# An opening stage written out in source order, with the weights loaded and converted earlier

## The chip, the cores and the metric

The kernel runs on one core of a Trainium2 chip. The metric is the time of one execution on the device, in microseconds (us). The core has five engines with a queue of instructions each: PE (the matrix engine), DVE (the vector engine), ACT (the scalar engine), POOL (the general engine) and SP, which here issues most of the DMA transfers. The engines run side by side and wait for one another by semaphores.

## The reference, cut to what matters

There are four batches of 12480 tokens of width 128. In each, 49 agent vectors attend to the keys and collect the values, and then each query attends to the 49 agents. The result, 49920 rows of 128, goes through a gated feed-forward layer of 2048 units.

```python
a2k = softmax(scale * agents @ k.T)        # 49 x 12480, per batch
agent_v = a2k @ v                          # 49 x 128
q2a = softmax(scale * q @ agents.T)        # 12480 x 49
x = (q2a @ agent_v).reshape(49920, 128)
h = x @ w_in                               # 128 -> 2048, weights in 64-bit floats
g = h * (1.0 / (1.0 + np.exp(-1.702 * h)))
out = (g @ w_out).astype(np.float32)       # 2048 -> 128
```

The weights come as 64-bit floats. [...]

## The kernel before, in words

**The main loop.** The tokens are taken 1000 at a time, in 50 groups; a group has 16 steps, one for each 128 units of the feed-forward layer. `two_steps(t)` does steps t and t+1: `up` (L437, L440) multiplies the softmax of the queries with a product of agent values and `w_in`, ACT applies the activation (L450), `high` rounds the result (a DMA cast issued by POOL, L456, or ACT or DVE), `low` takes the rest on DVE (L465), and `down` (L475), four steps later, multiplies both with `w_out`. Beside this, a table `at` holds jobs with the step at which each is due: for the next batches the loads, splits and scores of the keys and values, and for the next groups those of the queries. In the main loop PE, ACT, DVE and POOL carry out their work in the order of the source; only the SP queue is ordered by a planner, which takes, in the order of the source, what it holds to be ready.

**The opening.** Before the loop, the first batch has to be worked through, since the loop needs its agent values. Its order on all engines is the planner's. The keys come in 13 blocks of 960 tokens (L578) and get scored (`first_key_scores`, L236), ACT copies the scores out (L245), DVE keeps a running maximum (L252). `do_query_split` makes three 16-bit parts of the first 1000 queries on DVE (L183, L185). Then the maximum over all keys is taken (L259 to L276, with two transposes on PE), and it is subtracted from the scores block by block (`key_shift`, L291: the first on DVE, the twelve others on POOL), ACT takes the exponent (L295), and PE sums up the values (L616). The 13 blocks of values go into buffers that later hold weights; there is room for eight blocks, and each two more wait until the sums have read the buffer they go into. Scores, softmax and transposes of the first queries are `do_query_scores`, `do_query_shift`, `do_query_exp`, `do_query_sums`, `do_query_softmax`, `do_query_pairs` (L380 to L427).

**The weights.** `load_words` brings a block of 512 columns in 64-bit form, 512 KB, into one of three buffers that keys and values use later (tag `kv`); four blocks of `w_in` and four of `w_out` are needed. `to_float32` makes floats of a block by eight operations on DVE (L133 to L145). For `w_out`, ACT then makes a rounded copy (L154) and DVE the rest (L155). The buffer is free for the next block once the sixth operation has read it. `weights_part` (L350) multiplies the agent values with a block of `w_in`; ACT copies the product (L357), DVE takes the rest (L359), and six small DMA transfers (`move`, L366) put the rest where `up` wants it.

**What is in which order before.** SP issues the 13 key blocks, the first queries, two value blocks, the first `w_in` block, the eleven other value blocks, and then the other weights. The block of `w_in` that came in first is converted while POOL shifts the scores; the other seven are converted after the value sums and among the first steps of the main loop.

Of the kernel before, what the change touches and what calls it, by code (L numbers as in the profile page):

```python
# [35 lines left out]
V_AT = (6, 10, 14)  # L36
V_SLOTS = (3, 2, 2, 2, 2, 2)
R = 30
FIRST_WORDS = 1
FIRST_UP = 2  # L40
BOTH = (0,)
ON_DVE = (2,)
EPS = 1e-09
# [3 lines left out]
def kernel(  # L47
# [77 lines left out]
    def to_float32(w, out=None):  # L125
        lo = w[:, :, 0]
        hi = w[:, :, 1]
        ts = nc.vector.tensor_scalar
        stt = nc.vector.scalar_tensor_tensor

        tmp = work.tile([P, 2, 512], U32, name="tmp", tag="rest")
        ex = tmp[:, 0].bitcast(I32)
        ts(out=ex.bitcast(U32), in0=hi, scalar1=20, scalar2=0x7FF, op0=ALU.logical_shift_right, op1=ALU.bitwise_and)  # L133
        ts(out=ex, in0=ex, scalar1=1023 - 127, scalar2=1023 + 128, op0=ALU.max, op1=ALU.min)
        ts(out=ex, in0=ex, scalar1=float(127 - 1023), scalar2=float(1 << 23), op0=ALU.add, op1=ALU.mult)
        stt(out=ex.bitcast(U32), in0=hi, scalar=0x80000000, in1=ex.bitcast(U32), op0=ALU.bitwise_and, op1=ALU.bitwise_or)

        m = work.tile([P, 512], U32, name="m21", tag="o")
        r = tmp[:, 1]
        ts(out=m, in0=hi, scalar1=0xFFFFF, scalar2=0x100000, op0=ALU.bitwise_and, op1=ALU.bitwise_or)  # L140
        ts(out=r, in0=lo, scalar1=8, scalar2=None, op0=ALU.logical_shift_right)
        stt(out=m.bitcast(F32), in0=m, scalar=float(1 << 24), in1=r, op0=ALU.mult, op1=ALU.add)
        if out is None:
            out = m.bitcast(F32)
        stt(out=out, in0=m.bitcast(F32), scalar=2.0**-44, in1=ex.bitcast(F32), op0=ALU.mult, op1=ALU.mult)  # L145
        return out

    def up_weights(i, w):
        to_float32(w, w_in_sb[:, i * 512 : (i + 1) * 512])

    def down_weights(i, w):
        s = slice(i * 4, (i + 1) * 4)
        wo = to_float32(w).rearrange("p (f c) -> p f c", c=C)
        nc.scalar.copy(out=wo_h[:, s, :], in_=wo)  # L154
        nc.vector.tensor_sub(out=wo_l[:, s, :], in0=wo, in1=wo_h[:, s, :].bitcast(F32))  # L155

# [74 lines left out]
    def first_key_scores(g, kt):  # L231

        for c in range(2):
            ps = ps_m.tile([P, 512], F32, name="ps_m")
# [11 lines left out]
        running_max(g, score[:TB, g * KB : (g + 1) * KB, :])  # L246

    def running_max(g, s):
        if g == 0:
# [12 lines left out]
    def key_max_1(d):  # L262
        mx = d["mx"]
        ps = ps_m.tile([P, 512], F32, name="ps_m")
# [7 lines left out]
    def key_max_2(d):  # L272
        mrow = d["mrow"]
        ps = ps_m.tile([P, 512], F32, name="ps_m")
# [3 lines left out]
    def key_max():  # L278
        d = {}
        key_max_0(d)  # L280
        key_max_1(d)
        key_max_2(d)

    def value_load(b, g):
        t = loads.tile([P, KB, C], F32, name="vt", tag="kv")
# [64 lines left out]
    def weights_part(b, w, c):  # L350
        if c == 0:
            wts[b] = wpool.tile([P, F], F32R, name="wh"), wpool.tile([P, F], F32R, name="wq")
        wh, wq = wts[b]
        s = slice(c * 512, (c + 1) * 512)
        pw = ps_m.tile([P, 512], F32, name="ps_m")
        nc.tensor.matmul(out=pw, lhsT=w["avT"], rhs=w_in_sb[:, s], start=True, stop=True)  # L356
        nc.scalar.copy(out=wh[:, s], in_=pw)  # L357
        wl = work.tile([P, 512], F32R, name="wl")
        nc.vector.tensor_sub(out=wl[:A], in0=pw[:A], in1=wh[:A, s].bitcast(F32))  # L359
        move(wh[A:H, s], wl[0 : R // 2])  # L360
        move(wh[H + A : P, s], wl[R // 2 : R])
# [190 lines left out]
    def do_query_exp(n):  # L552
        if n < NG:
            query_exp(scored[n])
# [22 lines left out]
    for g, t in enumerate(first_keys()):  # L577
        nc.sync.dma_start(out=t, in_=kT[0, :, g * KB : (g + 1) * KB, :])  # L578
        kts[0, g] = t
    do_query_load(0)  # L580
    words_in = []
    for g in range(NKG):
        if g % 2 == 0:
            vt0 = wpool.tile([P, 2, KB, C + 1], F32, name="vt0", tag=("wh", "wq")[g // 2 % 2])
            nc.gpsimd.memset(vt0[:, :, :, C :], 1.0)
        vts[0, g] = vt0[:, g % 2]
        nc.sync.dma_start(out=vt0[:TB, g % 2, :, 0:C], in_=v[0, :, g * KB : (g + 1) * KB, :])
        if g == FIRST_WORDS:
            words_in.append(load_words(w_in, 0))
    words = []  # L590
    for i in range(NF // 4):
        if i:
            words_in.append(load_words(w_in, i))
        words.append(load_words(w_out, i))
    for g in range(NKG):
        first_key_scores(g, kts.pop((0, g)))
    for i in range(4):
        do_query_split(0, i)
    key_max()
    def ahead(n):  # L600
        for c in range(2):
            do_query_scores(n, c)
        do_query_load(n + 1)
        do_query_shift(n)
        do_query_exp(n)
        do_query_sums(n)

    ahead(0)
    do_query_softmax(0)
    acc_ps = ps_o.tile([P, 512], F32, name="po0")  # L610
    for g in range(NKG):
        key_shift(g, nc.vector.tensor_tensor if g == 0 else nc.gpsimd.tensor_tensor)
        key_exp(g, 1)
# [9 lines left out]
        if g == FIRST_UP:  # L623
            up_weights(0, words_in[0])
        if g == 6:
            do_query_pairs(0)
    accs[0] = work.tile([P, 2 * C + 1], F32, name="acc", bufs=1)
    nc.gpsimd.memset(accs[0], 0.0)
    nc.vector.tensor_copy(out=accs[0][:A, 0:C], in_=acc_ps[:A, 0:C])
    nc.vector.tensor_copy(out=accs[0][:A, 2 * C :], in_=acc_ps[:A, C : C + 1])  # L630
    w0 = {}
    weights_0(accs.pop(0), w0)
    weights_1(w0)
    for c in range(2):
        if c:
            up_weights(c, words_in[c])
        weights_part(0, w0, c)
    for i in range(4):
        do_query_split(1, i)
    ahead(1)  # L640
    do_query_softmax(1)
    down_weights(0, words[0])


    steps = NG * NF
# [11 lines left out]
        pe_steps.add(t)  # L657
        return t

    for i in range(1, NF // 4):  # L660
        if i > 1:
            put(4 * i - 8, lambda i=i: up_weights(i, words_in[i]))
            put(pe_step(4 * i - 6), lambda i=i: weights_part(0, w0, i))
        put((1, 4, 6)[i - 1], lambda i=i: down_weights(i, words[i]))
    exps = {}
    for b in range(B - 1):
        s0 = due[b] - due[b] % (2 * NF) if b else 0
        done = s0
        for k in range(NKG):
            t = s0 + (K_AT if b else K_FIRST)[k]  # L670
            assert pe_step(t) == t
            put(t - 13 if b else max(t - 13, 0), lambda b=b, k=k: do_key_load(b + 1, k))
# [53 lines left out]
        put(s0 + Q_AT + 1, lambda n=n: do_query_shift(n + 2))  # L726


    E = mybir.EngineType
    g = {}  # L730
    gh = {}
    gl = {}
# [51 lines left out]
    def do_low(u):  # L784
        gl[u] = low(g.pop(u), gh[u])

    with tc.manual_schedule(engines={E.PE, E.Activation, E.DVE, E.Pool}):
        for t in range(0, steps + LAG, 2):
            two_steps(t)
    assert not at  # L790


# [36 lines left out]
```

## Time and profile before

| what | value |
|---|---|
| time, median of 3 runs | 2001.62 us (2001.57 to 2003.75) |
| the profiled execution's own time | 1999.4 us |
| its span in the profile | 1997.6 us |
| busy: PE, DVE, ACT, POOL | 1954.9 (98%), 1628.0 (81%), 1425.6 (71%), 270.0 (14%) us |
| chain of work that ended last, by engine | PE 90%, DVE 4%, issue 3%, DMA 2% |
| first `up` of the main loop begins | 76.17 us |

Times in the profile count from the start of the span. A busy PE is not a PE at its peak. The granted clock is given as a share of full speed: 1.00 is 2.4 GHz and 0.50 is 1.2 GHz. From about 122 us on PE is busy almost without a gap; what comes before is the opening and the first steps of the main loop.

### The profile page before, as it was taken

The numbers are of one execution on the slowest core, as the hardware profiler recorded it, in microseconds if no ns is written. First come the engines' busy times: TensorE is split into PE (matmuls) and PEld (weight loads), VectorE is DVE, ScalarE is ACT, GpSimd is POOL, SyncE is SP. The second block draws the span as 40 slices with busy tenths as digits, with TensorE's granted clock in tenths as the row PEclk, the third lists the DMA queues.
The fourth block names the chain that finished last, engine by engine and source line by source line (L and its number), as shares of the span: only waits on it lengthen the run. The fifth ranks groups of instructions, "written<-read, shape, count | busy, mean of one in ns | idle before, by whom it ended". The sixth has DMA issues, their size and how long they took to land.

```text
span 1997.6 us, 33834 instructions
## 1 busy us (share of the span) xinstructions
PE 1954.9 (98%) x12464; PEld 1472.8 (74%) x12464; DVE 1628.0 (81%) x2069; ACT 1425.6 (71%) x2364; POOL 270.0 (14%) x574
## 2 busy tenths in 40 slices
PE   8689999999999999999999999999999999999999
PEld 7467777777777777777777777777777777777776
DVE  5799989888788889888879888988877767777675
ACT  3267777777767776776777777677777787777875
POOL 3011111111111111111111111111111111111111
PEclk9799999999999999999999999999999999999999
DMA  9556666655556665665546566565445555554543
GB/s 264 179 166 186 191 188 191 173 182 190 168 181 193 182 182 178 201 179 175 180 161 198 184 200 183 173 194 177 151 160 171 163 174 162 166 168 162 181 145 134
DMA packets 132777, 356.26 MB, mean 178 GB/s; under 512 B 15984, under 2 KB 60992, under 8 KB 132612
## 3 DMA queue, kind: packets, MB, share of 16 engines
q0 software_dynamic: 64928, 230.58, 35.3%
q1 hardware_dynamic: 67684, 123.52, 22.5%
q8 instruction: 98, 1.61, 0.3%
q14 instruction: 67, 0.55, 0.1%
HBM read 81.01 MB, written 25.56 MB: 53 GB/s over the span
## 4 chain that ended last, share of the span: by engine, by line
PE 90%; DVE 4%; issue 3%; DMA 2%; ACT 0%; POOL 0%; SPq 0%; ACTq 0%; POOLq 0%; DVEq 0%
PE po L475 53%; PE ph L437 17%; PE ph L440 8%; PE ps_m L196 3%; PE ps_m L310 2%; PE ps_m L410 1%; PE ps_m L236 1%; PE ps_m L215 1%; DMA gh<-g 1%; DVE gl L465 1%; PE ps_m L217 1%; PE po L616 1%; PE ps_m L356 1%; PE ps_m L218 0%; PE ps_m L216 0%
## 5 line engine op out<-in xcount | busy, mean ns | idle before, releaser
L450 ACT ACTIVATE g<-ph 128x500 f32<-128x500 f32 x1600 | 811.1, 594 | 467.5 <-PE ph L440 463.1
L465 DVE TENSOR_TENSOR gl<-g,gh 128x1000 fp32r<-128x1000 f32 x800 | 939.9, 1195 | 124.9 <-DMA gh<-g 79.7
L475 PE MATMUL po<-gh,wo_h 128*128 128x500 f32 x1600 | 533.2, 414 | 1.4 <-DMA gh<-g 1.4
L475 PE MATMUL po<-gl,wo_h 128*128 128x500 f32 x1600 | 494.6, 390 | 2.9 <-DVE gl L465 2.8
L475 PE MATMUL po<-gh,wo_l 128*128 128x500 f32 x1600 | 492.6, 389 | 0.0
L456 POOL DMA_DIRECT2D gh<-g x450 | 241.0, 535 | 1657.3 <-ACT g L450 1108.9
L475 PEld LDWEIGHTS po<-gl,wo_h 128*128 128x128 f32 x1600 | 301.0, 189 | 68.7 <-DVE gl L465 7.2
L475 PEld LDWEIGHTS po<-gh,wo_l 128*128 128x128 f32 x1600 | 301.6, 188 | 62.0
L475 PEld LDWEIGHTS po<-gh,wo_h 128*128 128x128 f32 x1600 | 272.5, 189 | 87.8 <-issue 55.1
L437 PE MATMUL ph<-sa,wh 128*128 128x500 f32 x800 | 314.4, 393 | 5.2 <-ACT g L450 4.3
L460 ACT CAST gh<-g 128x1000 fp32r<-128x1000 f32 x300 | 309.5, 1032 | 8.9
L437 PE MATMUL ph<-sb,wh 128*128 128x500 f32 x800 | 314.2, 393 | 0.0
L440 PE MATMUL ph<-rq,wq 19*128 19x500 f32 x1600 | 201.1, 491 | 0.0
L437 PEld LDWEIGHTS ph<-sa,wh 128*128 128x128 f32 x800 | 150.7, 188 | 43.0 <-ACT g L450 12.4
L440 PEld LDWEIGHTS ph<-rq,wq 19*128 19x128 f32 x1600 | 76.6, 182 | 139.1 <-issue 139.1
L437 PEld LDWEIGHTS ph<-sb,wh 128*128 128x128 f32 x800 | 150.6, 188 | 37.8 <-ACT g L450 6.9
L185 DVE TENSOR_TENSOR rest<-rest 128x508 bf16<-128x508 f32 (+3 forms) x178 | 129.7, 737 | 0.9
L422 DVE TENSOR_TENSOR sa<-ps_m,sa 49x500 fp32r<-49x500 f32 x50 | 33.6, 672 | 54.4 <-ACT sb L420 54.3
L183 DVE TENSOR_TENSOR rest<-qt 128x508 f32<-128x508 f32 x100 | 67.5, 677 | 0.0
L218 PE MATMUL ps_m<-ag_part,rest 128*128 128x49 bf16 x400 | 59.9, 187 | 3.7 <-DVE rest L185 3.7
L450 ACT ACT_TABLE_LOAD x49 | 62.9, 1283 | 0.9
L486 ACT COPY o<-po 128x500 f32<-128x500 f32 x100 | 53.9, 608 | 13.3 <-PE po L475 12.8
(102 smaller groups left out, 1598.8 us busy)
## 6 DMA issues: line engine op xcount, KB each, us to landing
gh<-g POOLq DMA_DIRECT2D x450, 500.0 KB, 4.4
qt<-qT SPq DMA_DIRECT2D x100, 250.0 KB
kt<-kT SPq DMA_DIRECT2D x52, 480.0 KB
vt<-v SPq DMA_DIRECT2D x52, 480.0 KB
outT<-o SPq DMA_DIRECT2D x96, 250.0 KB
rq<-sa SPq DMA_DIRECT2D x100, 37.1 KB
rq<-sb SPq DMA_DIRECT2D x100, 37.1 KB
sa<-sa SPq DMA_DIRECT2D x100, 29.3 KB
```

The costliest lines, as they stand in the source:

```text
L183: nc.vector.tensor_sub(out=r[:, s], in0=t[:, s], in1=halves(t)[0][:, s])
L185: nc.vector.tensor_sub(out=halves(r)[1][:, s], in0=r[:, s], in1=halves(r)[0][:, s])
L196: nc.tensor.matmul(out=o, lhsT=x[:, t], rhs=ag_part[:, b, y, :], start=(i == 0), stop=(i == len(products) - 1),)
L218: mm(out=o[:, 0:A], lhsT=x2[:, t], rhs=a[:, 0:A], start=False, stop=True)
L437: nc.tensor.matmul(out=ph[k][:, :CH], lhsT=wts[c][0][:, cols[i]], rhs=pairs[c], start=True, stop=False)
L440: nc.tensor.matmul(out=ph[k][:, :CH], lhsT=wts[c][1][r, cols[i]], rhs=rq[r], start=False, stop=True, tile_position=(k * 32, 0),)
L450: nc.scalar.activation(out=gs[i][:, c, :], in_=ph[k][:, :CH], func=AF.Gelu_apprx_sigmoid)
L456: nc.gpsimd.dma_start(out=gh, in_=g)
L460: nc.scalar.copy(out=gh, in_=g)
L465: nc.vector.tensor_sub(out=gl, in0=g, in1=gh.bitcast(F32))
L475: nc.tensor.matmul(out=po[c][:, :CH], lhsT=lhsT[:, f, :], rhs=rhs[:, c, :], start=(begin and first), stop=(end and last),)
L486: nc.scalar.copy(out=o, in_=po[c][:, :CH])
```

## The change

- The opening is written out in source order for PE, ACT, DVE and POOL. SP's queue stays with the planner.
- Three weight blocks (`w_in` 0, `w_out` 0, `w_in` 1) are loaded among the first keys, the first queries after the sixth key block. Eight value blocks are asked for next. `w_out` 1, `w_in` 2 and `w_out` 2 follow where the source comes to them (in the key loop after block 6 and after block 10, and behind the key loop), the last two blocks after the first weight products.
- `to_float32` becomes a generator that stops after each operation; `convert(n)` does the next n of them. In the key loop two or three go ahead of each running maximum, in the value loop four after each of the last five blocks, and the rest at steps 0 to 2 of the main loop.
- The first queries are split after the last four key blocks. Their scores go ahead of the two transposes of the maximum on PE.
- All 13 shifts are on DVE, two blocks ahead of the sums. Split, scores and softmax of the second 1000 queries move into the value loop.
- The moves of the first two weight products are issued from ACT's queue; before, SP issued them, and POOL four of them.
- The third weight product is at step 0, ahead of the conversions of that step; the fourth stays at step 6. The first key loads of the next batch are due at step 4 at the earliest.

```diff
+WORDS_AT = (1, 4, 7)
+Q_FIRST = 5
+PART_AT = (0, 0, 0, 6)
+CONVERT_AT = (8, 8, 6, 6, 4, 4, 4, 4, 4, 4, 4)
...
+    def convert(ops):
+        while ops and converting:
+            if next(converting[0], 0) is None:
+                ops -= 1
+            else:
+                converting.pop(0)
...
+        queue = nc.scalar if b == 0 and c < 2 else None
+        move(wh[A:H, s], wl[0 : R // 2], queue)
+        move(wh[H + A : P, s], wl[R // 2 : R], queue)
         for i in range(4):
-            move(wq[i * 32 : i * 32 + A - R, s], wl[R:A], None if b or c else nc.gpsimd)
+            move(wq[i * 32 : i * 32 + A - R, s], wl[R:A], queue)
...
+    def load_next_words():
+        i, c = divmod(len(words), 2)
+        w = load_words((w_in, w_out)[c], i)
+        words.append(w)
+        converting.append((up_weights, down_weights)[c](i, w))
...
+    def shift(g):
+        key_shift(g, nc.vector.tensor_tensor)
+        key_exp(g, 1)
...
+    with tc.manual_schedule(engines=in_order):
...
+        for g, t in enumerate(first_keys()):
+            nc.sync.dma_start(out=t, in_=kT[0, :, g * KB : (g + 1) * KB, :])
+            kts[0, g] = t
+            if g in WORDS_AT:
+                load_next_words()
+            if g == Q_FIRST:
+                do_query_load(0)
+        values = first_values()
+        for g in range(KB):
+            next(values)
+        for g in range(NKG):
+            first_key_scores(g, kts.pop((0, g)))
+            convert(2 + g % 2)
+            running_max(g, score[:TB, g * KB : (g + 1) * KB, :])
+            if g == 6:
+                load_next_words()
+            if g == 10:
+                load_next_words()
+            if g >= NKG - 4:
+                do_query_split(0, g - NKG + 4)
+        do_query_load(1)
+        load_next_words()
+        d = {}
+        key_max_0(d)
+        for c in range(2):
+            do_query_scores(0, c)
+        key_max_1(d, ps_h.tile([P, 512], F32, name="ph"))
+        key_max_2(d, ps_h.tile([P, 512], F32, name="ph"))
+        shift(0)
+        shift(1)
+        do_query_shift(0)
+        do_query_exp(0)
+        acc_ps = ps_o.tile([P, 512], F32, name="po0")
+        for g in range(NKG):
+            if g + 2 < NKG:
+                shift(g + 2)
+            first_sums(g)
+            if g < 5 and g + KB < NKG:
+                next(values)
+            if g == 0:
+                do_query_sums(0)
+                do_query_softmax(0)
+            elif g < 5:
+                do_query_split(1, g - 1)
+                if g == 2:
+                    do_query_pairs(0)
+            elif g == 5:
+                for c in range(2):
+                    do_query_scores(1, c)
+                do_query_load(2)
+            elif g == 6:
+                do_query_shift(1)
+                do_query_exp(1)
+            elif g == 7:
+                do_query_sums(1)
+                do_query_softmax(1)
+            if g > 7:
+                convert(4)
+        nc.vector.tensor_copy(out=accs[0][:A, 0:C], in_=acc_ps[:A, 0:C])
...
+        for c in range(2):
+            weights_part(0, w0, c)
+        while len(words) < 8:
+            load_next_words()
...
+    for c in range(2, F // 512):
+        put(pe_step(PART_AT[c]), lambda c=c: weights_part(0, w0, c))
+    for t, ops in enumerate(CONVERT_AT):
+        put(t, lambda ops=ops: convert(ops))
```

## Rows read from the trace of the kernel before

**Rows 1.** Busy time of each engine in three stretches: the first keys, the values, and from there to the steady loop. Columns: stretch, its length, then for PE, PEld, DVE, ACT and POOL the busy us and the instructions, and at the end the granted clock, the DMA share and GB/s.

```profile
0.00:30.00 30.00, 24.35 (x208) 24.21 (x208) 10.22 (x22) 9.59 (x27) 3.49 (x17) 1.00 0.99 307
30.00:65.00 35.00, 26.91 (x246) 25.91 (x246) 23.78 (x39) 8.42 (x17) 14.21 (x16) 0.95 0.98 210
65.00:122.00 57.00, 39.47 (x195) 25.33 (x196) 49.93 (x89) 23.90 (x41) 6.30 (x14) 0.70 0.49 147
```

**Rows 2.** What SP issued in the opening, in order of time. Columns: start, us until the last of the group was issued, queue, line, operation, transfer, count.

```profile
1.18 9.17 SPq L578 DMA_DIRECT2D kt<-kT  x13
...
13.64 4.08 SPq L587 DMA_DIRECT2D vt<-v  x2
17.77 3.34 SPq L122 DMA_DIRECT2D words<-w_in  x1
21.15 26.97 SPq L587 DMA_DIRECT2D vt<-v  x11
48.16 2.47 SPq L122 DMA_DIRECT2D words<-w_out  x1
```

**Rows 3.** What the transfers moved in some stretches of the opening. Columns: stretch, its length, granted clock, DMA share (1 is all sixteen engines busy), GB/s.

```profile
10.00:18.00 8.00, 1.00 1.03 413
...
20.00:24.00 4.00, 1.00 1.17 211
...
28.00:50.00 22.00, 0.92 1.11 198
...
56.00:58.00 2.00, 1.00 0.98 383
```

**Rows 4.** Instructions of the opening in order of time. Columns: start, us, engine, line, operation, out<-in, shape, count, and in brackets how long the engine was idle before and what ended that.

```profile
0.74 0.39 SPq L85 DMA_DIRECT2D ag_sb<-agT  x1
...
2.75 0.93 DVE L162 CAST ag_part<-ag_sb 128x196 bf16<-128x196 f32 x1 [1.75 <-DMA ag_sb<-agT]
...
31.78 0.80 DVE L259 TENSOR_REDUCE mx<-run_max 120x49 f32<-120x392 f32 x1
...
33.87 0.22 PE L215 MATMUL ps_m<-ag_part,qt 128*128 128x98 bf16 x1
...
33.98 0.21 DVE L276 COPY max_b<-ps_m 120x49 f32<-120x49 f32 x1 [0.41 <-PE ps_m L275]
...
35.63 0.24 PE L218 MATMUL ps_m<-ag_part,rest 128*128 128x49 bf16 x1
36.36 13.13 PE L616 MATMUL po<-vt,score 120*49 120x129 f32 x112 [0.49 <-ACT score L295]
...
50.00 10.83 PE L616 MATMUL po<-vt,score 120*49 120x129 f32 x96
```

**Rows 5.** The chain that ended last, in order of time: one weight block of `w_out` from its first operation on DVE to the last, with the rest taken after ACT's copy. Columns: start, us, engine, tile, line.

```profile
93.45 0.35 DVE tmp L133
...
96.87 0.70 DVE m L145
97.60 0.63 ACT wo_h L154
98.25 0.69 DVE wo_l L155
```

**Rows 6.** The same chain: a running maximum, two pieces of a query split, and one of the operations on 125x392 of a query's softmax.

```profile
30.17 0.49 DVE run_max L252
30.66 1.23 DVE rest L185 x2
...
75.32 0.57 DVE e_sb L380
```

**Rows 7.** Instructions from the end of the value sums to the first activation, in order of time; columns as in rows 4.

```profile
64.95 0.28 DVE L629 COPY acc<-po 49x128 f32<-49x128 f32 x1
...
68.65 0.28 DVE L344 TENSOR_TENSOR avT<-ps_m,rz 128x128 f32<-128x128 f32 x1
...
71.82 0.68 DVE L359 TENSOR_TENSOR wl<-ps_m,wh 49x512 fp32r<-49x512 f32 x1 [0.96 <-ACT wh L357]
...
78.08 1.28 ACT L450 ACT_TABLE_LOAD   x1
...
79.37 2.02 ACT L450 ACTIVATE g<-ph 128x500 f32<-128x500 f32 x4
```

**Rows 8.** The line that issues the moves: what one issue takes on SP, ns min/median/max.

```profile
L366 SPq DMA_DIRECT2D wq<-wl x60: 564/572/865, 76.0 to 1496.6; - x60
L366 SPq DMA_DIRECT2D wh<-wl x32: 783/838/2061, 72.5 to 1490.1; - x32
```

**Rows 9.** PE in the main loop: the first matmul of `up` at steps 0, 6, 8, 12 and 22; columns as in rows 4.

```profile
76.17 0.47 PE L437 MATMUL ph<-sa,wh 128*128 128x500 f32 x1 [0.89 <-DMA wh<-wl]
...
94.09 0.39 PE L437 MATMUL ph<-sa,wh 128*128 128x500 f32 x1
...
109.62 0.39 PE L437 MATMUL ph<-sa,wh 128*128 128x500 f32 x1
...
121.93 0.39 PE L437 MATMUL ph<-sa,wh 128*128 128x500 f32 x1
...
145.89 0.38 PE L437 MATMUL ph<-sa,wh 128*128 128x500 f32 x1
```

**Rows 10.** DMA issues by line: the casts that POOL issues, count, KB each, median us from issue to landing.

```profile
gh<-g POOLq DMA_DIRECT2D x450, 500.0 KB, 4.4
```

More of the change, by code (lines that the diff above doesn't have):

```diff
@@ L145, in to_float32 @@
         stt(out=out, in0=m.bitcast(F32), scalar=2.0**-44, in1=ex.bitcast(F32), op0=ALU.mult, op1=ALU.mult)
+        yield
         return out
     def up_weights(i, w):
-        to_float32(w, w_in_sb[:, i * 512 : (i + 1) * 512])
+        yield from to_float32(w, w_in_sb[:, i * 512 : (i + 1) * 512])
     def down_weights(i, w):
         s = slice(i * 4, (i + 1) * 4)
-        wo = to_float32(w).rearrange("p (f c) -> p f c", c=C)
+        wo = yield from to_float32(w)
+        wo = wo.rearrange("p (f c) -> p f c", c=C)
         nc.scalar.copy(out=wo_h[:, s, :], in_=wo)
         nc.vector.tensor_sub(out=wo_l[:, s, :], in0=wo, in1=wo_h[:, s, :].bitcast(F32))
+        yield
+    words = []
+    converting = []
+    def convert(ops):
[4 more added lines that the diff above has]
+                converting.pop(0)
     ag_part = const.tile([P, B, 3, A], BF16, name="ag_part")
@@ L233, in first_key_scores @@
         for c in range(2):
-            ps = ps_m.tile([P, 512], F32, name="ps_m")
+            ps = ps_h.tile([P, 512], F32, name="ph")
             for j in range(KB // 2):
@@ L260, in key_max_0, with key_max_1 @@
         d["mx"] = mx
-    def key_max_1(d):
+    def key_max_1(d, ps=None):
         mx = d["mx"]
-        ps = ps_m.tile([P, 512], F32, name="ps_m")
+        if ps is None:
+            ps = ps_m.tile([P, 512], F32, name="ps_m")
         nc.tensor.transpose(out=ps[:A, :TB], in_=mx[:TB], identity=ident[:TB, :TB])
@@ L575, in first_keys, with first_values, first_sums @@
         return tiles[:NKG]
[L577 to L613, printed above, removed]
+    def first_values():
+        for g in range(NKG):
+            if g % 2 == 0:
+                vt0 = wpool.tile([P, 2, KB, C + 1], F32, name="vt0", tag=("wh", "wq")[g // 2 % 2])
+                nc.gpsimd.memset(vt0[:, :, :, C :], 1.0)
+            vts[0, g] = vt0[:, g % 2]
+            nc.sync.dma_start(out=vt0[:TB, g % 2, :, 0:C], in_=v[0, :, g * KB : (g + 1) * KB, :])
+            yield
+    def load_next_words():
[3 more added lines that the diff above has]
+        converting.append((up_weights, down_weights)[c](i, w))
+    def first_sums(g):
         vt = vts.pop((0, g))
@@ L622 @@
             )
[L623 to L630, printed above, removed]
-    w0 = {}
[L632 to L642, printed above, removed]
+    def shift(g):
+        key_shift(g, nc.vector.tensor_tensor)
+        key_exp(g, 1)
+    E = mybir.EngineType
+    in_order = {E.PE, E.Activation, E.DVE, E.Pool}
+    w0 = {}
+    with tc.manual_schedule(engines=in_order):
+        accs[0] = work.tile([P, 2 * C + 1], F32, name="acc", bufs=1)
+        nc.gpsimd.memset(accs[0], 0.0)
+        for g, t in enumerate(first_keys()):
[31 more added lines that the diff above has]
+        acc_ps = ps_o.tile([P, 512], F32, name="po0")
+        for g in range(NKG):
+            if g + 2 < NKG:
[23 more added lines that the diff above has]
+        nc.vector.tensor_copy(out=accs[0][:A, 0:C], in_=acc_ps[:A, 0:C])
+        nc.vector.tensor_copy(out=accs[0][:A, 2 * C :], in_=acc_ps[:A, C : C + 1])
+        weights_0(accs.pop(0), w0)
+        weights_1(w0)
+        for c in range(2):
+            weights_part(0, w0, c)
+        while len(words) < 8:
+            load_next_words()
@@ L658, in pe_step @@
         return t
[L660 to L664, printed above, removed]
+    for c in range(2, F // 512):
+        put(pe_step(PART_AT[c]), lambda c=c: weights_part(0, w0, c))
+    for t, ops in enumerate(CONVERT_AT):
+        put(t, lambda ops=ops: convert(ops))
     exps = {}
@@ L671 @@
             assert pe_step(t) == t
-            put(t - 13 if b else max(t - 13, 0), lambda b=b, k=k: do_key_load(b + 1, k))
+            put(t - 13 if b else max(t - 13, 4), lambda b=b, k=k: do_key_load(b + 1, k))
             begin = max(t - 4, done + 1)
@@ L785, in do_low @@
         gl[u] = low(g.pop(u), gh[u])
-    with tc.manual_schedule(engines={E.PE, E.Activation, E.DVE, E.Pool}):
+    with tc.manual_schedule(engines=in_order):
         for t in range(0, steps + LAG, 2):
             two_steps(t)
-    assert not at
+    assert not at and not converting
 _INS = ["qT", "kT", "v", "agT", "w_in", "w_out"]
```

23 lines of the change are left out of this document (10 added, 13 removed).

## The prediction

> **What bounds the kernel now.** I read first the share of the chain of waits and the granted clock along the span in the page, which say that from 122 us on PE is the limit; nothing of the change is there. Then the busy time by stretch [rows 1]. While the first keys are scored, PE is busy 24.4 of 30 us and DVE 10.2. From 65 to 122 us it is turned round: DVE is busy 49.9 of 57 us, PE 39.5 at a mean clock of 0.70. Two gaps of PE show the price: `up` of step 6 begins at 94.09 and that of step 8 at 109.62 us, where later two steps take under five (121.93 to 145.89 is ten steps) [rows 9]. What DVE does there is mostly the conversion of seven weight blocks: 4.12 us for the eight operations of one (93.45 to 97.57), and 0.69 us more for `w_out`, after a wait of about 0.65 us for ACT's copy [rows 5]. So there is something to win: DVE's idle time among the first keys. Whether it is won depends on the weights being there, so I went on to the list of SP's issues and the rates of the transfers. They show a queue that is full: values move at 198 to 211 GB/s, half of the 413 GB/s of the keys, at a DMA share over 1 from 20 to 50 us [rows 3]. And a block waits its turn: SP came to the first `w_out` block, which had a free buffer from the start, only after the last value block, at 48.16 us [rows 2].
>
> **When the weights arrive.** Before, keys and first queries fill the transfers until about 20.0 us, where the rate drops [rows 3]. Three blocks of 0.524 MB at 383 GB/s add 4.1 us: the values begin at 24.1. The next eight transfers in source order are value blocks of 0.492 MB, ready from the start, so I take it that the planner leaves them there; at 198 GB/s they take 19.9 us, to 44.0. The fourth weight block, `w_out` 1, stands behind them: 1.4 us, and about 1.6 us until its reader can begin (the agents' 98 KB were issued at 0.74 and used at 2.75, of which some 0.3 us is moving them [rows 4]). It is there at **47.0 us**.
>
> **When DVE wants it.** The key loop converts 2 or 3 operations per block: 25 after the tenth block, which is exactly blocks 0 to 2 (8 + 9 + 8). The next one, ahead of the eleventh maximum, is the first of `w_out` 1. DVE comes to it early: from 12.1 us, where two blocks are scored, there are 20 operations at 0.515 us, one rest with its wait (1.3), eight maxima at 0.49 and a split piece at 0.65 [rows 5, 6], together 16.2 us: 28.3 us. In source order, DVE then stands still for **18.7 us**, and behind it stand the last three maxima, three pieces of the first split, and so the maximum over all keys; ACT, PE's sums and the second queries wait for that.
>
> After 47.0 there are still seven operations (3.42), three maxima (1.5) and three pieces (2.05): 54.0. The first queries' scores, now ahead of the transposes, take 2.0 us (33.87 to 35.87), the rest of the maximum 1.5 (from the end of the first reduction to 34.19) [rows 4]: the maximum stands at 57.5 instead of 34.19. First term: **+23.3 us**. Nothing hides it, for PE has nothing left to score.
>
> **From the maximum to the end of the value sums.** Before, 34.19 to 64.95, 30.8 us [rows 4, 7]. Afterwards PE has 24.0 us of sums (13.13 + 10.83 [rows 4]) and some 2 of transposes and scores, DVE more: 13 shifts at 0.5 (6.5; I take the price of a maximum of the same shape, and at most the 1.3 us that an operation cost when POOL worked beside it, which it no longer does), two softmaxes of six operations at 0.5 and a short one (6.5), the rest of the pairs (1.3), the second split (2.6), and 19 operations of conversion with two waits (11.6): 28.5, and about 2.3 for waits for the exponent and PE. Sum 30.8. Second term: **0**, and the accumulator is copied at 88.3. The POOL shifts that go had been beside PE's sums, so their absence gives nothing.
>
> **From there into the loop.** Before: 64.95 to the activation at 79.37 is 14.4 us, to `up` of step 22 at 145.89 it is 80.9 [rows 7, 9]. Afterwards:
> - The first rest is ready after 6.9 us, 0.65 earlier (no conversion between). Then ACT issues six moves, two at 0.84 and four at 0.57 on SP [rows 8]: 4.0 us; copies the second product (1.3 with its rest), issues six more (4.0), loads its table (1.28): the first activation at 17.6, 3.2 us later than before. No row shows an issue by ACT; between nothing (-3.8 us at the end) and SP's longest of 0.87 and 2.06 (7 us more) I take SP's median, the nearest row.
> - The third product's copy stands behind the four activations (2.0), and DVE's rest of it ahead of all conversions: 20.9. Then sixteen operations (8.2), ACT's copy and the rest (1.3): 30.5. Only then the `low` of steps 0, 1 and 3, at 1.1 us each, and a cast (0.67) come; `down` of steps 0 and 1 is done at some 37, two of its four halves at half clock. `up` of step 6 begins 37.2 after the accumulator, 8 us later than before (29.1).
> - Against this the gap at step 6 is gone, since nothing is left to convert: step 8 at 42.4 (before 44.7), step 12 at 52.3 (57.0), step 22 at 75.8 (80.9). From there on PE does the same as before.
>
> Third term: **-5.1 us**.
>
> One rule speaks of this place. A DMA that POOL issues lands in 4.4 us at the median [rows 10], and I let the casts of steps 0 and 1 land beside the conversions. The Trainium skill (SBUF — State Buffer, "SBUF: two separate sides") says that POOL can't write its descriptors while a DVE copy runs in a two-port mode; by it the casts would start only after the sixteen operations and land about 2 us after the time at which I use them, and the sum would be +20 rather than +18. No row of before shows a cast held up so, and I add nothing.
>
> **Sum.** +23.3 + 0 - 5.1 = +18.2. The profiled execution took 1999.4 us (its span 1997.6), so 2017.6; the median of the runs lies 2.2 above it, so **2019 us** for the median, rounded down because the issues by ACT may be cheaper. The forecast's own range is 2010 to 2027: -4 for free issues and -5 for waits I counted twice, +8 for longer ones.
>
> **Rivals.**
> - *The block isn't queued behind the values.* The planner could put `w_out` 1 earlier, as source order once put a `w_in` block behind two value blocks [rows 2]; in at 29.3 us it would cost no stall. Then the maximum stands at 39.8 (+5.6: 32 conversion operations, 16.5 us, don't fit into DVE's 20 idle us together with the waits for scores, and the scores go first). The second queries, loaded once the first scores have read their buffer, land at about 51 behind the values, and DVE waits 4 to 5 us for them: accumulator at 76, +11 in all, less 5.1: +6, 2007 us. For it: the planner is free on SP. Against: values come first in the source and wait for nothing. Chance 0.11.
> - *Faster: nothing stalls.* Everything as in the first rival, the second queries come in time too, and PE's 26 us of sums and scores set the end: accumulator at 67 (+2); with ACT's issues free, -5.1 and -3.8: -7, about 1995 us. It decides at one point: `w_out` 1 in its buffer before 28 us. For it: DVE's idle time is there. Against: the queue's rates. Chance 0.18.
> - *The stall is there and the loop makes it good*: the value sums hide the conversions, the first steps run without waits. That takes 13 us that no row offers; with the cases between the last two it has 0.06, within 0.2%.
>
> **How the numbers follow.** Forecast 0.65, rivals 0.11, 0.18, 0.06. A measurement tells 0.2% (4 us) from no change. Slower: the forecast and the first rival, 0.76, plus a little of the last: 0.77; same 0.05; faster 0.18. The range reaches down through the first rival and the cases near no change, and leaves out the faster one and a tail above: 1999 to 2028.
>
> **What would show it.** Right: DVE idle for 15 to 20 us from about 28 us on before a L133, ended by the DMA of `w_out`; the copy of the maximum (L276 before) at 55 to 59 us; the accumulator at 85 to 91; ACT's twelve issues between 92 and 106; `up` of step 6 at 120 to 127 and of step 22 at 158 to 168, with PE without gaps from step 8. Wrong: the maximum before 42 us, or a weight block of `w_out` among the first value blocks in SP's list; then the first term falls. Issues of ACT at 0.1 us would take 3 to 4 us off the last term, and a `low` that waits for a DMA while conversions run would add to it.

## The result, and the profile after

The changed kernel takes **2027.49 us** (median of 4 runs, 2026.09 to 2029.21); the kernel before took 2002.38 beside it. The ratio is 1.0125 with a 95% interval of 1.0108 to 1.0143: slower by 25 us. The profiled execution took 2027.94 us with a span of 2026.1, 28.5 more than the span before; the profiled execution of the kernel before was a short one (1999.4 us, 3.0 under the median beside it), so differences of spans come out some 3 us larger here than those of medians.

In the new line numbers L135 is the first operation of a conversion, L376 the rest of a weight product, L384 a move, L455 and L458 are the two kinds of matmul of `up`, L613 the value sums, L689 the copy of the accumulator. The windows of rows 1, for the kernel after:

```profile
0.00:30.00 30.00, 24.59 (x209) 24.48 (x210) 20.64 (x44) 9.85 (x27) 3.48 (x17) 1.00 0.98 326
30.00:65.00 35.00, 9.10 (x64) 7.98 (x63) 14.87 (x31) 3.30 (x7) 0.00 (x0) 0.56 0.68 153
65.00:122.00 57.00, 40.06 (x260) 29.56 (x258) 32.49 (x66) 15.72 (x29) 2.20 (x7) 0.83 0.51 124
```

DVE now works 20.6 of the first 30 us instead of 10.2, as the change means it to. The second row is the price: PE falls from 26.9 to 9.1 us at a granted clock of 0.56 (between the two levels, 1.2 and 2.4 GHz), and DVE from 23.8 to 14.9. The timeline of SP, in answer to rows 2, and that of DVE (columns as in rows 4) say why:

```profile
16.36 23.31 SPq L601 DMA_DIRECT2D vt<-v  x8
39.79 2.22 SPq L124 DMA_DIRECT2D words<-w_out  x1
...
56.18 0.81 SPq L391 DMA_DIRECT2D qt<-qT  x2
```

```profile
48.62 0.43 DVE L135 TENSOR_SCALAR tmp<-words 128x512 uint32<-128x512 uint32 x1 [20.74 <-DMA words<-w_out]
...
57.53 0.21 DVE L299 COPY max_b<-ph 120x49 f32<-120x49 f32 x1 [0.49 <-PE ph L298]
...
69.31 0.67 DVE L440 TENSOR_TENSOR sa<-ps_m,sa 49x500 fp32r<-49x500 f32 x1 [4.14 <-ACT sb L438]
...
91.64 0.28 DVE L689 COPY acc<-po 49x128 f32<-49x128 f32 x1
```

Eight value blocks go ahead of `w_out` 1, SP comes to it at 39.8 us, and DVE stands 20.7 us for it, from 27.9 to 48.6. The maximum stands at 57.74 instead of 34.19 [rows 4]. The main loop, in answer to rows 9, as PE's timeline has it (the first matmul of steps 0, 6, 8, 12, 14 and 22, with three of the matmuls of step 12):

```profile
100.99 0.76 PE L455 MATMUL ph<-sa,wh 128*128 128x500 f32 x1 [4.35 <-DMA wh<-wl]
...
127.14 0.38 PE L455 MATMUL ph<-sa,wh 128*128 128x500 f32 x1
...
132.25 0.39 PE L455 MATMUL ph<-sa,wh 128*128 128x500 f32 x1
...
141.96 0.39 PE L455 MATMUL ph<-sa,wh 128*128 128x500 f32 x1
...
143.98 0.49 PE L458 MATMUL ph<-rq,wq 19*128 19x500 f32 x1 [0.53 <-DMA wq<-wl]
146.65 0.48 PE L458 MATMUL ph<-rq,wq 19*128 19x500 f32 x1 [2.17 <-DMA wq<-wl]
148.53 0.78 PE L458 MATMUL ph<-rq,wq 19*128 19x500 f32 x1 [1.40 <-DMA wq<-wl]
...
155.26 0.39 PE L455 MATMUL ph<-sa,wh 128*128 128x500 f32 x1
...
173.91 0.39 PE L455 MATMUL ph<-sa,wh 128*128 128x500 f32 x1
```

Steps 12 to 14 take 13.3 us, where before they took about 5.3. The four narrow moves of the fourth weight product, 19 rows each, were issued by SP from 133.6 to 136.1, and the last of them is in only at 148.5. After step 22 both kernels take the same time (1852.2 and 1851.7 us to the end), so all of the loss stands ahead of it:

| stretch | before | after | change | forecast |
|---|---|---|---|---|
| start to the maximum | 34.19 | 57.74 | +23.55 | +23.3 |
| to the accumulator | 30.76 | 33.90 | +3.14 | 0 |
| to `up` of step 12 | 56.98 | 50.32 | -6.66 | -4.7 |
| step 12 to step 22 | 23.96 | 31.95 | +7.99 | -0.4 |
| sum, to step 22 | 145.89 | 173.91 | +28.02 | +18.2 |

### The profile page after: what moved, and what is told of

It reads as the page before. It is cut to its first block, busy times and chain, and to the rows that moved or that the text cites. A ratio compares the mean times of both kernels' runs of the same rounds, so it can differ in the third digit from the quotient of the medians.

```text
span 2026.1 us, 33819 instructions
## 1 busy us (share of the span) xinstructions
PE 1959.6 (97%) x12464; PEld 1475.2 (73%) x12464; DVE 1629.6 (80%) x2081; ACT 1426.1 (70%) x2364; POOL 255.4 (13%) x558
## 4 chain that ended last, share of the span: by engine, by line
PE 88%; DVE 4%; issue 3%; DMA 3%; SPq 1%; ACT 1%; POOL 0%; ACTq 0%; POOLq 0%; DVEq 0%
PE po L493 53%; PE ph L455 17%; PE ph L458 8%; PE ps_m L218 2%; PE ps_m L327 2%; PE ps_m L428 1%; SPq L601 1%; PE ps_m L237 1%; DMA wq<-wl 1%; PE ps_m L239 1%; DMA kt<-kT 1%; DVE gl L483 1%; DMA gh<-g 1%; PE po L613 1%; PE ps_m L240 0%
## 5 line engine op out<-in xcount | busy, mean ns | idle before, releaser
L455 PE MATMUL ph<-sa,wh 128*128 128x500 f32 x800 | 315.3, 394 | 5.0 <-DMA wh<-wl 4.3
L455 PE MATMUL ph<-sb,wh 128*128 128x500 f32 x800 | 314.4, 393 | 0.0
L458 PE MATMUL ph<-rq,wq 19*128 19x500 f32 x1600 | 205.6, 490 | 9.1 <-DMA wq<-wl 9.1
L458 PEld LDWEIGHTS ph<-rq,wq 19*128 19x128 f32 x1600 | 78.4, 182 | 151.6 <-issue 139.1
L455 PEld LDWEIGHTS ph<-sa,wh 128*128 128x128 f32 x800 | 150.9, 189 | 42.7 <-ACT g L468 7.6
L455 PEld LDWEIGHTS ph<-sb,wh 128*128 128x128 f32 x800 | 151.0, 189 | 38.1 <-ACT g L468 6.7
L504 ACT COPY o<-po 128x500 f32<-128x500 f32 x100 | 53.9, 609 | 13.3 <-PE po L493 13.0
```

What stands on the lines that cost most here:

```text
L455: nc.tensor.matmul(out=ph[k][:, :CH], lhsT=wts[c][0][:, cols[i]], rhs=pairs[c], start=True, stop=False)
L458: nc.tensor.matmul(out=ph[k][:, :CH], lhsT=wts[c][1][r, cols[i]], rhs=rq[r], start=False, stop=True, tile_position=(k * 32, 0),)
L504: nc.scalar.copy(out=o, in_=po[c][:, :CH])
```

## The experiments

Each edit is made to the changed kernel, unless another is named. Times are medians; those of the kernel before lay between 2001.35 and 2002.51 us beside them. The theory: three causes that add up (the weight block behind the values, the moves on ACT's queue at step 0, the narrow moves of the later products). The rivals: the conversions don't fit among the keys at all, whenever their block comes; the place of the third product at step 0 is the cost.

### The weight block behind two value blocks

```diff
-        for g in range(KB):
+        for g in range(2):
             next(values)
...
-            if g == 6:
+            if g == 3:
                 load_next_words()
+            if 3 <= g < 9:
+                next(values)
```

> The change with one thing moved: the fourth weight block (w_out 1) is asked for behind two value blocks and not behind eight. Queue theory (the vector engine stands still from 27.9 to 48.6 us only because this block lies behind eight value blocks in a full queue): the block lands at 29 to 32 us, the stand shrinks from 20.7 us to under 4, the maximum over the keys stands at 40 to 44 instead of 57.7, and of that 14 to 17 us some are lost again because the second queries and the last value blocks come late: total 8 to 15 us less than the changed kernel. Rival (the conversions are simply too much work among the keys): the stand goes but the maximum stays after 50 us, total within 4 us of the changed kernel.

Measured: 2014.67 us, ratio 1.006 (1.0045 to 1.0075; all ratios are to the kernel before), 13 us less than the change. DVE's timeline:

```profile
34.98 0.43 DVE L135 TENSOR_SCALAR tmp<-words 128x512 uint32<-128x512 uint32 x1 [7.90 <-DMA words<-w_out]
...
43.88 0.21 DVE L299 COPY max_b<-ph 120x49 f32<-120x49 f32 x1 [0.48 <-PE ph L298]
...
52.31 0.69 DVE L205 TENSOR_TENSOR rest<-qt 128x508 f32<-128x508 f32 x1 [2.51 <-DMA qt<-qT]
```

The stall shrinks from 20.7 to 7.9 us, the maximum comes 13.7 us earlier and the end 12.8: what the stall costs reaches the end almost in full. The time came as expected, the landing did not: the block is there at 35.0 us instead of 29 to 32, and the stall is not under 4. A small wait for the second queries, which stand behind the values too, is new.

### The fourth block is not converted among the keys

```diff
-            convert(2 + g % 2)
+            if g < 10:
+                convert(2 + g % 2)
```

> The change without the conversions ahead of the last three running maxima: the seven operations of the fourth block that stood there move behind (into the value loop and the first steps). The order of the transfers stays. Queue theory: the wait goes from the key stage, the maximum stands at 36 to 40 us instead of 57.7; the second queries, asked for behind the values, then hold the vector engine for some us, and the seven operations come back later: total 8 to 16 us less than the changed kernel. Rival (the transfers themselves bound the stage): the wait turns up again in full at the second queries or at the values, total within 4 us of the changed kernel.

Measured: 2014.49 us, ratio 1.0059 (1.0042 to 1.0075). Here nothing waits for the block, and DVE's timeline shows the next in line:

```profile
34.02 0.21 DVE L299 COPY max_b<-ph 120x49 f32<-120x49 f32 x1 [0.41 <-PE ph L298]
...
51.52 0.69 DVE L205 TENSOR_TENSOR rest<-qt 128x508 f32<-128x508 f32 x1 [11.59 <-DMA qt<-qT]
```

With three blocks converted among the keys the maximum stands at 34.2 us, just where it stood before: these 25 operations are free. But 23 us of gain end as 13, because the second queries land behind the values at 51.5, and their split stands ahead of the other shifts on DVE. The stall had hidden a second stall.

### The moves as before

```diff
-        queue = nc.scalar if b == 0 and c < 2 else None
+        queue = None
...
-            move(wq[i * 32 : i * 32 + A - R, s], wl[R:A], queue)
+            move(wq[i * 32 : i * 32 + A - R, s], wl[R:A], None if b or c else nc.gpsimd)
```

> The change with the moves of the first two weight products issued as in the kernel before (the narrow wq moves of the first product by GpSimd, all others by SP). Theory of the narrow moves (a transfer of 19 rows issued by ACT or SP runs as 19 packets one behind the other, so four of them take 7 us; GpSimd spreads them): the four wq matmuls of step 0 end about 3 us after the first up matmul instead of 8, step 6 comes 4 to 6 us earlier, total 3 to 7 us less. Rival (ACT's time for twelve issues is what costs, as the prediction had it): the activations of step 0 come 3 to 4 us earlier and the wq matmuls still wait 0.8 us for one another. Second rival: GpSimd's and SP's issues are as late, no change.

Measured: 2021.6 us, ratio 1.0096 (1.0081 to 1.0111), 6 us less. From the accumulator to step 12 it takes 45.6 us instead of 50.3; of the rest 1.3 us were won ahead of the accumulator, where the edit changes nothing. Step 2 follows step 0 after 3.75 us (100.34 to 104.09) instead of 9.15 (100.99 to 110.14). With ACT's queue, the four narrow matmuls of step 0 had each waited for a move of their own, 0.55, 0.84, 0.82 and 0.79 us, the last until 108.34, though the moves had all been issued by 102.1; with GpSimd issuing them no such wait is left. But the run takes away two things that end almost together in the kernel after: the last of these matmuls begins at 108.34, and ACT issues the second product's moves until 108.73, with three activations of step 0 behind them (108.78). So the rival, that ACT's time for its issues costs, isn't ruled out, and the run with the moves cut in two shows it at work. The stand at step 12 stays.

### The narrow moves of the third and fourth product by GpSimd

```diff
-            move(wq[i * 32 : i * 32 + A - R, s], wl[R:A], queue)
+            move(wq[i * 32 : i * 32 + A - R, s], wl[R:A], nc.gpsimd if b == 0 and c > 1 else queue)
```

> The change with the narrow wq moves of the third and fourth weight product issued by GpSimd instead of SP. Theory of the narrow moves: the stand of the matrix engine in step 12 (wq matmuls waiting until 148.5 us) goes, step 12 to step 14 takes 5 to 6 us instead of 13.3, total 7 to 9 us less. Rival (the transfers of that time, casts and key blocks, fill all engines): the wq matmuls of step 12 wait as before, total within 2 us; GpSimd's casts may come later by the four issues, 2 us.

Measured: 2019.58 us, ratio 1.0086 (1.0071 to 1.0101), 8 us less, close to the 8.0 of the table. Steps 12 and 14 in PE's timeline:

```profile
142.49 0.39 PE L455 MATMUL ph<-sa,wh 128*128 128x500 f32 x1
147.85 0.39 PE L455 MATMUL ph<-sa,wh 128*128 128x500 f32 x1
```

The two steps take 5.36 us, and the moves that GpSimd issued landed 2.1 to 3.3 us after their issue. Step 12 itself comes 1.5 us later after the accumulator than in the kernel after (51.8 for 50.3), and the accumulator 0.9 earlier.

### The same queues, but each narrow move cut in two

```diff
-            move(wq[i * 32 : i * 32 + A - R, s], wl[R:A], queue)
+            if b:
+                move(wq[i * 32 : i * 32 + A - R, s], wl[R:A])
+            else:
+                move(wq[i * 32 : i * 32 + 16, s], wl[R : R + 16], queue)
+                move(wq[i * 32 + 16 : i * 32 + A - R, s], wl[R + 16 : A], queue)
```

> The change with each narrow wq move of the first batch (19 rows) cut into one of 16 and one of 3 rows, on the same queues: twice as many issues, the same bytes. Theory of the narrow moves (a transfer of 19 rows, which is a prime, is carried by one transfer engine, one of 16 rows by sixteen): the wq matmuls of step 0 no longer wait 0.8 us for one another, and the stand in step 12 goes: step 12 to 14 takes 5 to 7 us instead of 13.3; ACT issues eight more times (5 us), which eats the gain at step 0. Total 5 to 10 us less than the changed kernel. Rival (small transfers issued by SP and ACT are late whatever their rows, or their number counts): step 12 to 14 stays at 13 us or grows, total the same or up to 10 us more.

Measured: 2023.31 us, ratio 1.011 (1.0096 to 1.0124), 4 us less, a little under what was expected. The view of the tile `wq` counts how long its readers and writers stood, and for what (a matmul and its weight load each count); first the kernel after, then this one, both from 95 to 150 us:

```profile
L384 ACTq DMA_DIRECT2D wq<-wl x8: 591/594/642, 99.5 to 108.1; - x8
L384 SPq DMA_DIRECT2D wq<-wl x8: 564/577/1212, 114.8 to 135.5; - x8
its engine sat idle before it (us, times) until:
  DMA wq<-wl: 21.6, 16
```

```profile
L388 ACTq DMA_DIRECT2D wq<-wl x16: 559/641/737, 98.1 to 111.3; - x16
L388 SPq DMA_DIRECT2D wq<-wl x16: 554/655/837, 116.6 to 141.7; - x16
its engine sat idle before it (us, times) until:
  DMA wq<-wl: 3.3, 4
```

The same bytes by the same queues in twice as many moves: the waits go from 21.6 to 3.3 us, and steps 12 to 14 take 5.36 us. The share of the sixteen transfer engines' time that SP's queue took (packets, MB, share) shows the difference, first in the kernel after from 143 to 148.5 us, then here from 137.1 to 142.4, while the narrow moves of the fourth product run:

```profile
q1 hardware_dynamic: 46, 0.09, 5.1%
```

```profile
q1 hardware_dynamic: 158, 0.17, 13.6%
```

One engine's whole time would be 6.25%, so the uncut moves got no more than one engine's worth, the cut ones more than two. The trace's packet records say the same: in the kernel after the four moves' packets of 2,048 bytes run one at a time from 138.4 to 147.9 us, 84 ns each at the shortest. Until 138.3 the query moves in front of them on SP's queue, of 19 rows too, run in the same way. So what makes these moves slow on the queues of SP and ACT is that they have 19 rows; neither their issue nor the other traffic does it alone. The Trainium skill ("DMA: Bandwidth & Descriptors", "Why a DMA increments its semaphore by 16 and not by 1") has the rule: such a transfer is spread over the largest number of engines up to 16 that divides its rows, which is one for 19 rows and sixteen for 16; from GpSimd it may be spread unevenly over more. The waits of the three runs and the two shares agree with it; how GpSimd's moves were spread no row here shows. The eight more issues on ACT take back a part: 0.64 us each, and step 6 comes at 129.88 instead of 127.14. ACT issues until 112.0, its three activations of step 0 come only then, and PE stands 4.67 us for them in step 2 (until 112.69): that is the rival named at the run with the moves as before, ACT's time for its issues.

### The three together, and then the second queries

The early block of the first run, and all narrow moves of the first batch by GpSimd, the wide ones on SP:

```diff
-        queue = nc.scalar if b == 0 and c < 2 else None
+        queue = None
...
-            move(wq[i * 32 : i * 32 + A - R, s], wl[R:A], queue)
+            move(wq[i * 32 : i * 32 + A - R, s], wl[R:A], None if b else nc.gpsimd)
```

> The change with three things together: the fourth weight block asked for behind two value blocks, all narrow moves of the first batch by GpSimd, the others by SP. If the three losses are apart in time, as the theories have it (13, 6 and 8 us one by one), they add up: 25 to 28 us less than the changed kernel, so 2000 to 2003 us, the same as the kernel before. Rival (they overlap, one is hidden behind the other): 2005 us or more.

Measured: 2001.36 us, ratio 0.9996 (0.9987 to 1.0006), 26 us less than the change; 13 + 6 + 8 = 27 were the parts. So the parts add up, and without them the change is as fast as the kernel before.

Next, `w_out` 1 goes ahead of all value blocks, and the second queries are asked for on ACT's queue, behind the first scores:

```diff
-        for g in range(2):
-            next(values)
...
-            if 3 <= g < 9:
+            if 3 <= g < 11:
                 next(values)
...
-        do_query_load(1)
         load_next_words()
...
             do_query_scores(0, c)
+        do_query_load(1, nc.scalar)
```

> As the three together, and the fourth weight block ahead of all value blocks, and the second queries asked for on ACT's queue, so that they don't lie behind the value blocks on SP's. Queue theory: the vector engine's waits for the fourth block (7.9 us when it lay behind two value blocks) and for the second queries (2.5 to 11.6 us) go; the maximum stands at 38 to 41 us, the accumulator is copied at 68 to 72 instead of 77.5 us: another 5 to 9 us less, 1992 to 1997 us. Rival (the values, now later, set the end of the sums): accumulator no earlier than 75 us, 2000 us or more.

Measured: 1998.06 us, ratio 0.9983 (0.9974 to 0.9992). The stall for the block is 1.08 us, the maximum at 37.99, but the accumulator only at 74.31, not at the 68 to 72 expected, and the time is 1 us above the expected 1992 to 1997: PE now waits 5.14 us for the last values (69.19). The rival was partly right.

### The third product behind the conversions

```diff
-PART_AT = (0, 0, 0, 6)
+PART_AT = (0, 0, 2, 6)
```

> As the run before, with the third weight product at step 2 instead of step 0. Theory (the vector engine stands for 8.4 us at step 0, because the rest of the third product is ahead of the last sixteen conversions and waits for ACT's copy behind the activations): the conversions begin 8 us earlier, the first low is done about 6 us earlier, step 6 comes 3 to 7 us earlier, total 3 to 7 us less than without: 1987 to 1993 us. Rival (step 6 waits for the activations, not for the conversions): within 2 us.

Measured: 2000.13 us, ratio 0.9992 (0.9984 to 1.0001): 2 us more than the kernel it is made from, not less. DVE's timeline has the reason:

```profile
65.90 0.42 DVE L135 TENSOR_SCALAR tmp<-words 128x512 uint32<-128x512 uint32 x1
75.27 0.43 DVE L135 TENSOR_SCALAR tmp<-words 128x512 uint32<-128x512 uint32 x1 [8.94 <-DMA words<-w_in]
...
82.03 0.28 DVE L689 COPY acc<-po 49x128 f32<-49x128 f32 x1
```

Two first operations of a conversion stand one behind the other: the first conversion of the main loop has moved in among the opening's last, ahead of the accumulator's copy, and waits there for its block. The opening and the main loop are two written-out sections, and the planner keeps the order within each, not across the border. Where the third product came first on DVE in the loop, it had held the border, since it needs the agent values; moved away, it no longer does. So this run says nothing of the product's place. The next one makes one section of both:

```diff
-PART_AT = (0, 0, 0, 6)
+PART_AT = (0, 0, 2, 6)
...
-    with tc.manual_schedule(engines=in_order):
+    written_out = tc.manual_schedule(engines=in_order)
+    written_out.__enter__()
...
-    with tc.manual_schedule(engines=in_order):
-        for t in range(0, steps + LAG, 2):
-            two_steps(t)
+    for t in range(0, steps + LAG, 2):
+        two_steps(t)
+    written_out.__exit__(None, None, None)
```

> As the version with the second queries' own queue (1998.1 us), but the third weight product is at step 2, and the opening and the main loop are one written-out section, so that DVE's order is the source's throughout (in the run before this, DVE's list had let the conversion of w_in block 2 in ahead of the accumulator's copy). Theory: what the third product costs at step 0 is DVE's wait of 8.2 us for ACT's copy behind four activations, with sixteen conversions behind it. Behind them the wait is gone: the conversions begin at about 81 instead of 89.5 us, the accumulator stays at 74 to 75, step 12 comes 41 to 43 us after it (45.9 with the product at step 0) and the time is 2 to 5 us shorter: 1993 to 1996. Rival: the word blocks for these conversions are the limit (SP asks for them at 67.4 and 67.9 us), the wait of DVE stays and only changes its name to a DMA: 1997 to 1999.

Measured: **1993.17 us**, ratio 0.9961 (0.9947 to 0.9975). DVE's timeline:

```profile
75.34 0.28 DVE L690 COPY acc<-po 49x128 f32<-49x128 f32 x1 [4.27 <-PE po L613]
...
80.20 1.50 DVE L376 TENSOR_TENSOR wl<-ps_m,wh 49x512 fp32r<-49x512 f32 x2 [1.94 <-ACT wh L374]
...
93.52 0.68 DVE L376 TENSOR_TENSOR wl<-ps_m,wh 49x512 fp32r<-49x512 f32 x1 [3.54 <-ACT wh L374]
```

The rest of the third product now stands behind the conversions; a wait of 8.2 us ahead of them has become one of 3.5 behind them. So the rival on the third product's place holds too, as a fourth cause. The single section came with the move, and the section alone was not run; that it alone changes nothing is argued from DVE's order, which was the source's already with the product at step 0. The accumulator comes 1 us later than in the version with the product at step 0, but step 12 comes 38.8 us after it instead of 45.9.

Last, values 11 and 12 are asked for on ACT's queue:

```diff
+            queue = nc.scalar if g > 10 else nc.sync
-            nc.sync.dma_start(out=vt0[:TB, g % 2, :, 0:C], in_=v[0, :, g * KB : (g + 1) * KB, :])
+            queue.dma_start(out=vt0[:TB, g % 2, :, 0:C], in_=v[0, :, g * KB : (g + 1) * KB, :])
```

> As the version in one section, and the last two value blocks are asked for on ACT's queue. There SP asked for them at 61.4 and 61.9 us, behind eight small moves of the first pair (issued from 53.7 to 61.3), and PE waited 5.1 us for them at 69.2. Theory: the blocks are late because of SP's order, not because the transfers are full: asked for 5 to 6 us earlier, they are in by about 65, PE's wait goes, and DVE's last conversion in the value loop (71.6 us) sets the accumulator, at 72 to 73 instead of 74.3: 1.5 to 2.5 us shorter than the version in one section. Rival: the transfers are the limit (their share is 0.95 to 1.1 up to 60 us): the blocks land as before or push another one back, no gain within 0.5 us.

Measured: **1989.97 us**, ratio 0.994 (0.9928 to 0.9953), the fastest of all. By the medians 3.2 us are gained, by the spans (1990.3 and 1988.5) 1.8; of the latter 1.5 stand at the accumulator. ACT issued the two blocks at 50.99 and 54.55, 7 to 10 us earlier than SP did, and PE's timeline shows what became of its waits:

```profile
60.58 1.94 PE L614 MATMUL po<-vt,score 120*49 120x129 f32 x16 [0.52 <-DMA vt<-v]
...
65.45 8.38 PE L614 MATMUL po<-vt,score 120*49 120x129 f32 x48 [2.93 <-DMA vt<-v]
```

The wait of 5.7 us is one of 2.9 and stands for an earlier block: theory and rival each hold half, and the accumulator misses the expected 72 to 73. In this version the accumulator is copied at 73.87, 8.9 us later than before, and step 22 begins 62.8 us after it instead of 80.9: 18.1 - 8.9 = 9.2, against 9.1 between the spans.

## Why the prediction was right or wrong

The direction and the main cause, the stall, were right; the time lies 8.5 us above the forecast, just above the forecast's own range of 2010 to 2027 and inside the wider one, which ends at 2028. Going by its steps:

- *When the weights arrive, when DVE wants it.* Right. The block was forecast in at 47.0, DVE at it at 28.3 and the maximum at 57.5; it was 48.6, 27.9 and 57.74. The term came out at +23.55 for +23.3. That it fits to 0.3 us is luck: the block came 1.6 us later than forecast, and what stands behind it up to the maximum took 9.1 us instead of 10.5. The early block shows that it is this wait that costs, and the run with three blocks that the conversions as such cost nothing among the keys. The first rival (the block not behind the values) did not come about: SP issued all eight value blocks first.
- *From the maximum to the end of the value sums.* Mis-sized: +3.14 for 0. DVE's work was 26.8 us, less than the 28.5 counted, but its waits ahead of the copy were 4.14, 0.72, 0.69 and 0.68, not 2.3. The largest is for ACT's copy of the first pairs, which wait for PE. PE began the sums with 48 matmuls in 8.48 us, 0.177 each, where the 112 of rows 4 took 0.117: it had stood for 20.4 us up to 50.7, and from 59 to 65 us the granted clock was 0.50, the lower level, against 0.96 over the 112. The forecast took the durations of a PE that had not stood. In the run with the moves as before the clock was at 1.00 from 63 us on, the same 48 took 7.20, that wait was 2.86 and the stretch 32.6: 1.3 less wait, 1.3 less time.
- *From there into the loop.* Up to step 12 right in sign, 2 us better than forecast (-6.66 for -4.7). Two errors work against each other in it. The first activation came 12.7 us after the accumulator, not 17.6, because it stands ahead of the second product's moves on ACT, not behind them; the three others of step 0 stand behind them. And ACT took 4.9 us for the first product's six issues and 4.3 for the second's, where 4.0 were counted, which is inside the bounds, but the moves then landed one by one, and step 2 came 9.15 us after step 0.
- *"From there on PE does the same as before."* This sentence failed, and with it the sign of the term: step 12 to step 22 was 8.0 us longer. The same four moves on SP had done no harm before: SP had issued them by 111.1, and their first matmul came at 122.93, 11.8 us later. Now the steps run faster towards them: step 12 is where their matmuls come, 7 us earlier after the accumulator, the first matmul follows the last issue by 6.9 us, and moves that come in one behind the other, the last 12.4 us after its issue, are not in yet. The prediction counted what it takes to issue a move and never what it takes to land, though it asked of every other transfer when it is in. Cutting the moves, or having GpSimd issue them, takes the stand away.
- *The rule on POOL's DMAs beside DVE's copies* was weighed and left out of the sum. POOL issued casts at 109.67, 110.63 and 114.70, the conversions ran from 112.4 to 120.7, and the casts' packets of 4,000 bytes moved between 110 and 118 us, beside them; the first `low` (121.97) then began right behind the last conversion. No start only after the sixteen operations is to be seen; that the hold would last over all sixteen was the prediction's own step. The casts did land later, at a median of 7.5 us for the four issued from 105 to 125 against 4.4 [rows 10]; whether the conversions had a part in that isn't shown.
- *The rival "faster: nothing stalls"* named the block in its buffer before 28 us as its condition. The version with a stall of 1.08 us all but meets it and shows that it isn't enough: the second queries, the last values and the third product's place each stood behind it, and only with all of them moved do the 1990 us come, near the 1995 it named.

## What to carry to other kernels

Work that is moved into another engine's idle time is only as early as its data: before filling a gap, write down for each block when its transfer is asked for, behind which bytes, and when it is wanted, and do so for everything that stands behind it in the same queue. A transfer that was harmless behind a slow step has to be looked at again once the step is fast, and small ones by when they land, not by what their issue takes. Where one stall is removed, expect the next in line at once (here the weights, then the queries, the last values, a product's place): three fixes of 6 to 13 us and three of 3 to 5 turned a loss of 25 us into a gain of 12.

## What had not been expected of the hardware

- A move of 19 rows of 2,048 bytes is much slower than its 38 KB suggest. The four of one product, issued within 2.5 us, were all in only at 148.5 us, 12.4 behind the last issue, some 2 of them behind other moves of 19 rows; in two moves of 16 and 3 rows, or issued by GpSimd, the stand of PE disappears.
- An issue on ACT's queue takes 0.59 us at the median for a narrow move and 0.84 for a wide one, much as on SP [rows 8], and ACT's own work stands behind it: 4.3 us for the second product's six, ahead of three activations.
- Blocks on a second queue need not wait for all that the first has in front of it: two value blocks issued on ACT's queue at 51.0 and 54.6 us, where SP came to them from 61.1 on, brought the accumulator 1.5 us forward, with the transfers busy all the while (share 1.10 from 30 to 65 us).
